# One store for each output row tile in place of two, and a later place for one pair's query sums, in an attention and FFN kernel

## The chip, the cores and the metric

One core of one Trainium2 chip. The metric is the device time of one execution in microseconds (us). A run that is over 1.5% above the fastest of its kernel is called slow and is left out of every ratio.

The span that a profile gives is some 1.8 us shorter than the time of the same run, because it goes from the first instruction to the last only. Differences of spans and differences of times can be put beside each other.

## The reference, cut to what matters

```python
# q, k, v: [8 batches, 8 heads, 1152, 64] f32
q_pool = q.reshape(B, H, S // 2, 2, D).mean(axis=3)           # 576 queries
attn   = softmax(q_pool @ k.T / 8)                            # 576 x 1152 for each head
x      = (attn @ v).transpose(0, 2, 1, 3).reshape(4608, 512)  # 8 x 576 tokens
out    = ((x @ w1) * (x @ w2)) @ w3 @ w_out                   # [4608, 512] f32
```

## The kernel before

The attention goes through the heads in 32 pairs, numbered from 0. For each pair TensorE forms the scores (`psc`, line 315), ScalarE the exponentials (`er`, line 325), and TensorE sums them with the values (`po`, line 340). VectorE divides (`xn`, line 357) and a DMA transposes the result into `xT` (lines 365 and 368). The keys and queries of pairs 8 to 31 come to TensorE by DMA transposes too: `kT<-kc` (line 145) and `qT<-qp` (line 148); those of pairs 0 to 7 are transposed by TensorE. All the DMA transposes are issued from SyncE, whose queue is called SP below. The loads of `q`, `k` and `v` are issued from GpSimd, but for the keys and queries of pair 0.

The second half of the reference runs in 9 units of 512 tokens. Seven of them are interleaved with the attention, so that TensorE has work while ScalarE is at the exponentials; two come at the end, with `tail` set. A unit forms two products (`pa`, `pb`, line 434), multiplies them (`gT`, line 446), and multiplies by `w3 @ w_out`, which is formed once (`T16`; `pp`, line 452). Then come four row tiles of 128 tokens: an eviction from the accumulator to `osb`, and a store.

The tokens of a batch are not in the order of the output's rows. Token `64*c + p` of a batch is output row `9*p + c`. So 64 neighbouring tokens go to rows that lie 9 apart, and a tile of 128 tokens is two such groups, `c` and `c + 1`. A tile that starts at token 512 of 576 reaches into the next batch.

```python
def rows(i, o, n):                      # columns o to o+n of row tile i of unit t
    def mm(p, ft):
        nc.tensor.matmul(p[:, 0:n], gT[:, ft, 128*i:128*i + 128], T16[:, ft, o:o + n],
                         start=(ft == 0), stop=(ft == NF - 1))
    def end(p):
        if o == 0:
            osbs[i] = ffp.tile([128, dm], FP32, tag="osb", bufs=6, name="osb")
        ...                             # evict p to osb, on ScalarE or VectorE
        if not final and o + n < dm:
            return
        cs = slice(o, o + n) if final else slice(0, dm)
        for z in range(2):
            b, f = divmod(t0 + 128*i + 64*z, SQ)
            dst = out[b*SQ:(b + 1)*SQ, :].rearrange("(p c) m -> c p m", c=NJ)
            eng = nc.scalar if final and z else nc.sync
            eng.dma_start(out=dst[f // 64][:, cs], in_=osbs[i][64*z:64*z + 64, cs])
    final = t == n_units - 1 and i == 3
    ...
for i in range(4):
    last = t == n_units - 1 and i == 3
    widths = (256, 128, 128) if last else (512,) if tail else (256, 256)
    ...

# in the loop over steps, where pairs 1 to 7 get their sums and copies on VectorE:
    if 5 <= staged < NPE and it >= first_it(staged) - 3:   # ahead of the step's matmul groups
        prep_stage(staged)                                 # qp = even + odd queries; kc = copy of keys
    ...                                                    # the groups of this step
    if staged < 5 and it >= first_it(staged) - 2:          # after them
        prep_stage(staged)
```

The softmax here doesn't subtract the row's maximum and nothing guards it: scores larger than these inputs give would overflow.

Of the kernel before, what the change touches and what calls it, by code (L numbers as in the profile page):

```python
# [14 lines left out]
SQ = 576  # L15
NJ = 9
# [7 lines left out]
def kernel(  # L24
# [11 lines left out]
    nc = tc.nc  # L36
    B, H, S, D = q.shape
    dm = H * D
# [6 lines left out]
    NPE = 8  # L45
# [13 lines left out]
    T16 = const.tile([128, NF, dm], FP16)  # L59
# [39 lines left out]
    def load(P):  # L99
        if P < NP:  # L100
            load_k(P)
            load_q(P)
            load_v(P)
# [32 lines left out]
    def prep_dma(P):  # L136

        pool_q(P, 2)
        for p in (P, P + 1):
            new_kq(p)  # L140
            nc.gpsimd.tensor_copy(  # L141
                out=new_kc(p).rearrange("p j u d -> p u j d").bitcast(mybir.dt.int32),
                in_=kst.pop(p).bitcast(mybir.dt.int32))
        for p in (P, P + 1):
            nc.sync.dma_start_transpose(
                out=kT[p], in_=kcs[p].rearrange("p j u d -> p (j u d)"))
            if p == P:
                nc.sync.dma_start_transpose(
                    out=qTs[P // 2], in_=qps[P // 2].rearrange("p c u d -> p (c u d)"))
# [12 lines left out]
    def prep_stage(P):  # L162

        pool_q(P)
        nc.vector.tensor_copy(out=new_kc(P).rearrange("p j u d -> p u j d"), in_=kst.pop(P))
# [135 lines left out]
    def scores(c):  # L301
        t = psum.tile([128, 2, CH], FP32, tag="psc", bufs=3, name="psc")
        psc[c] = t
        if 3 <= c < 10:
            nc.tensor.matmul(t[:, 0], ones[:, 0:128], ones, start=True, stop=True)
        g = c * CH
        while g < (c + 1) * CH:
            J = g // SQ
            P, j = divmod(J, NJ)
            f0 = g - J * SQ  # L310
            ln = min(SQ - f0, (c + 1) * CH - g)
            o = g - c * CH
            for u in range(2):
                s = slice(64 * u, 64 * u + 64)
                nc.tensor.matmul(t[:, u, o:o + ln].rearrange("p (c f) -> p c f", f=64), kT[P][s, j, :],  # L315
                                 qT[P][s, f0 // 64:(f0 + ln) // 64], start=True, stop=True)
            g += ln

    def expo(c):
        r = (c * CH) % RING  # L320
        g = (c - RING // CH + 1) * CH
        if g > 0:
            Pg, Jg = divmod((g - 1) // SQ, NJ)
            assert nb >= 90 * Pg + 45 + 5 * Jg + 5
        nc.scalar.activation(out=er[:, :, r:r + CH], in_=psc.pop(c), func=AF.Exp,  # L325
                             bias=0.0, scale=SCALE)
# [69 lines left out]
    tail = False  # L396
# [28 lines left out]
    def ffn_groups(t):  # L425
        t0 = 512 * t
        gT = ffp.tile([128, NF, 512], FP16, tag="g", name="gT")
        asb = {}

        def half(ft, name):  # L430
            w = w1sb if name == "pa" else w2sb

            def mm(p, mc):
                nc.tensor.matmul(p, w[:, mc, ft * 128:ft * 128 + 128],  # L434
                                 xT[:, mc, t0:t0 + 512],
                                 start=(mc == 0), stop=(mc == NC - 1))

            def end(p):
                if name == "pa":
                    asb[ft] = ffp.tile([128, 512], FP32, tag="asb", name="asb")  # L440
                    if tail:
                        nc.scalar.copy(out=asb[ft], in_=p)  # L442
                    else:
                        nc.vector.tensor_copy(out=asb[ft], in_=p)  # L444
                else:
                    nc.vector.tensor_mul(out=gT[:, ft, :], in0=p, in1=asb.pop(ft))  # L446
            return name, FP32, NC, mm, end

        def rows(i, o, n):

            def mm(p, ft):
                nc.tensor.matmul(p[:, 0:n], gT[:, ft, 128 * i:128 * i + 128],  # L452
                                 T16[:, ft, o:o + n],
                                 start=(ft == 0), stop=(ft == NF - 1))

            def end(p):
                if o == 0:
                    osbs[i] = ffp.tile([128, dm], FP32, tag="osb", bufs=6, name="osb")
                osb = osbs[i][:, o:o + n]
                if tail and not (final and o):  # L460
                    nc.scalar.activation(out=osb, in_=p[:, 0:n], func=AF.Copy, bias=0.0,  # L461
                                         scale=1.0 / (SCL * SCL))
                else:
                    nc.vector.tensor_scalar_mul(out=osb, in0=p[:, 0:n],  # L464
                                                scalar1=1.0 / (SCL * SCL))
                if not final and o + n < dm:
                    return
                cs = slice(o, o + n) if final else slice(0, dm)
                for z in range(2):
                    b, f = divmod(t0 + 128 * i + 64 * z, SQ)  # L470
                    dst = out[b * SQ:(b + 1) * SQ, :].rearrange("(p c) m -> c p m", c=NJ)
                    eng = nc.scalar if final and z else nc.sync
                    eng.dma_start(out=dst[f // 64][:, cs], in_=osbs[i][64 * z:64 * z + 64, cs])
            final = t == n_units - 1 and i == 3
            return "pp", FP32, NF, mm, end

        osbs = {}
        for ft in range(NF):
            yield half(ft, "pa")
            yield half(ft, "pb")  # L480
        for i in range(4):
            last = t == n_units - 1 and i == 3
            widths = (256, 128, 128) if last else (512,) if tail else (256, 256)
            for x, n in enumerate(widths):
                yield rows(i, sum(widths[0:x]), n)


    NCHUNK = NP * PAIR // CH
# [6 lines left out]
        out=ident, in_=ident, compare_op=ALU.not_equal, fill=1.0,  # L495
# [16 lines left out]
    loaded, staged, prepped, copied = 8, 1, 1, 1  # L512
# [24 lines left out]
    n_units = NT // 512  # L537
# [37 lines left out]
    def first_it(P):  # L575
        return P * PAIR // (CH * BURST)
# [21 lines left out]
    for it in range(NIT):  # L598
        at = it * BURST * CH / PAIR
        while early and it >= early[0][0]:  # L600
            queue.append(early.pop(0)[1])
        while next_unit < EARLY:
            last_b = (512 * (next_unit + 1) - 1) // SQ
            if it < 3 or reached[it - 2] < 360 * (last_b + 1):
                break
            gens.append(ffn_groups(next_unit))
            next_unit += 1
        for w in range(BURST):
            if it == 0 and w == 2:
                some()  # L610
            if it == 1 and w == 1:
                rest()
            scores(BURST * it + w)
            expo(BURST * it + w)
        if 5 <= staged < NPE and it >= first_it(staged) - 3:
            prep_stage(staged)
            staged += 1
        while 8 <= loaded < NPE + 2 and at >= loaded - 3.4:
            load(loaded)
            loaded += 1  # L620
        urgent = False
        if prepped < NPE:
            if it >= first_it(prepped) - (1 if prepped < 5 else 2):
                queue[0:0] = prep_groups(prepped)
                prepped += 1
                urgent = True
        elif prepped < NP and at >= prepped - 1.95:
            prep_dma(prepped)
            if loaded < NP:
                settled(prepped)  # L630
                load_two(loaded)
                loaded += 2
            prepped += 2
        if NPE <= copied < NP and at >= copied - 1.1:
            copy_v(copied)
            copied += 1
        n = PVS[it]
        left = 45 - nb % 45
        brief = bool(queue) and queue[0][2] == 1
        a = left if left < n else 8 if brief and it > 8 and 8 < n < 40 and 8 < left < 45 else 0  # L640
        assert nb + n <= NPV and ready(nb + n - 1, BURST * it)
        pv(a)
        if head():
            group("F")
        if head() and (n < 40 or urgent or it < 17):
            group("X")
        pv(n - a)
        if staged < 5 and it >= first_it(staged) - 2:
            prep_stage(staged)
            staged += 1  # L650
            more_loads(staged)
        if copied < NPE and at >= copied + (0.25 if copied < 5 else 0):
            copy_v(copied)
            copied += 1
        reached.append(nb)
# [6 lines left out]
    tail = True  # L662
# [36 lines left out]
```

## Time and profile before

| | before |
|---|---|
| time, median (lowest to highest) of the 3 runs there were at the prediction | 419.31 us (418.67 to 420.48) |
| span of the profiled run | 416.7 us |
| TensorE busy, from all of the span | 406.1 us, 97% |
| end of TensorE's last matmul | 411.28 us |
| stores of output, and their size | 73 from SP, 3 from ScalarE; 128 KB, fewer columns at the end |

TensorE bounds this kernel: it idles for 5.1 us in the first 110 us, in waits of at most 0.8 us each, for 0.02 us from there to 411.28, and then 5.4 us pass in which the last rows leave. The "DMA" row of the page gives the busy share of the 16 DMA engines in tenths.

### The profile page before, as it was taken

To read this page: it belongs to the slowest core of one execution; us is meant where nothing else is said; L and a number is where in the kernel's file an instruction comes from. 1 tells how busy PE (TensorE), PEld (TensorE's weight loads), DVE (VectorE), ACT (ScalarE), POOL (GpSimd) and SP (SyncE) were. 2 spreads that over 40 slices of the span, in tenths; PEclk is the share of its full clock that TensorE was granted. 3 is DMA by queue.
4 is the path that set the end of the run, shared out by engine and by line. 5 is a ranking of instruction groups with operands and counts; after the bars stand their busy time and mean duration, and the time that the engine had idled before them with its cause. 6 is when DMAs were issued, how large, how long until landed. Compare 5 with 4: busy or idle time off the path is not lost.

```text
span 416.7 us, 12724 instructions
## 1 busy us (share of the span) xinstructions
PE 406.1 (97%) x5497; PEld 270.6 (65%) x5497; DVE 197.1 (47%) x408; ACT 326.0 (78%) x356; POOL 120.9 (29%) x161
## 2 busy tenths in 40 slices
PE   8999999999999999999999999999999999999994
PEld 5677777766775577666856786668656866544442
DVE  3546666455445543544455644554555345613130
ACT  5999999889888899888888889898888998032331
POOL 6533431343535255243525205243430000000000
PEclk9999999999999999999999999999999999999999
DMA  8999999799999999999799949998993341050404
GB/s 199 202 203 192 188 205 195 113 158 154 155 189 205 178 172 180 185 149 182 147 216 143 167 92 197 137 161 146 192 183 62 56 78 31 2 116 2 101 2 102
DMA packets 96489, 59.76 MB, mean 143 GB/s; under 512 B 65584, under 2 KB 86704, under 8 KB 96432
## 3 DMA queue, kind: packets, MB, share of 16 engines
q0 software_dynamic: 26928, 32.97, 50.8%
q1 hardware_dynamic: 69264, 25.84, 36.5%
q8 instruction: 43, 0.70, 0.7%
q10 hardware_dynamic: 240, 0.13, 0.1%
q14 instruction: 14, 0.11, 0.1%
HBM read 67.11 MB, written 9.44 MB: 184 GB/s over the span
## 4 chain that ended last, share of the span: by engine, by line
PE 85%; DMA 10%; ACT 2%; POOL 1%; issue 1%; DVE 1%; ACTq 0%; POOLq 0%
PE po L340 19%; PE psc L315 17%; PE pa L434 16%; PE pp L452 16%; PE pb L434 15%; DMA qst<-in_q_dram 7%; DMA w3h<-in_moe_w_dram 2%; ACT er L325 2%; PE pT L418 2%; DMA er<-in_k_dram 1%; POOL kst L88 1%; PE t L169 0%; POOL vst L95 0%; DVE qp L121 0%; POOL qst L81 0%
## 5 line engine op out<-in xcount | busy, mean ns | idle before, releaser
L325 ACT ACTIVATE er<-psc 128x1024 f16<-128x1024 f32 x324 | 307.2, 1029 | 41.2 <-PE psc L315 41.1
L340 PEld LDWEIGHTS <-er 128*128 128x128 f16 x2880 | 103.3, 97 | 22.0 <-issue 5.9
L340 PE MATMUL po<-vt,er 128*128 128x65 f16 x2880 | 110.3, 193 | 0.0
L315 PE MATMUL psc<-qT,kT 64*128 64x512 f16 (+7 forms) x1152 | 95.0, 285 | 3.4 <-ACT er L325 2.0
L446 DVE TENSOR_TENSOR gT<-pb,asb 128x512 f16<-128x512 f32 x72 | 49.8, 691 | 56.0 <-PE pb L434 55.4
L434 PE MATMUL pa<-xT,w1sb 128*128 128x512 f16 x288 | 74.2, 380 | 0.0
L434 PE MATMUL pb<-xT,w2sb 128*128 128x512 f16 x288 | 74.1, 380 | 0.0
L452 PE MATMUL pp<-T,gT 128*128 128x256 f16 (+2 forms) x496 | 67.9, 290 | 0.0
L315 PEld LDWEIGHTS <-kT 64*128 64x128 f16 x1152 | 45.5, 94 | 28.2 <-issue 9.4
L452 PEld LDWEIGHTS <-gT 128*128 128x128 f16 x496 | 45.9, 98 | 18.4 <-issue 3.7
L444 DVE COPY asb<-pa 128x512 f32<-128x512 f32 x56 | 38.7, 691 | 39.7 <-PE pa L434 38.6
L434 PEld LDWEIGHTS <-w2sb 128*128 128x128 f16 x288 | 26.4, 98 | 32.7 <-issue 3.9
L434 PEld LDWEIGHTS <-w1sb 128*128 128x128 f16 x288 | 25.1, 98 | 30.1 <-issue 6.2
L121 POOL TENSOR_TENSOR qp<-qst 128x1152 f16<-128x1152 f16 x12 | 28.3, 2354 | 54.2 <-issue 28.2
L464 DVE TENSOR_SCALAR osb<-pp 128x256 f32<-128x256 f32 (+1 forms) x50 | 21.0, 419 | 39.0 <-PE pp L452 38.7
L353 DVE RECIPROCAL rz<-po 128x5 f32<-128x5 f32 x64 | 12.4, 194 | 48.0 <-PE po L340 47.6
L357 DVE TENSOR_TENSOR xn<-po,rz 128x320 f16<-128x320 f32 x64 | 31.5, 492 | 2.2
L141 POOL COPY kc<-kst 128x576 int32<-128x576 int32 x24 | 16.2, 677 | 54.4 <-issue 42.0
L95 POOL DMA_DIRECT2D vst<-in_v_dram x32 | 23.4, 742 | 13.7 <-DMA w3h<-in_moe_w_dram 4.3
L461 ACT ACTIVATE osb<-pp 128x512 f32<-128x512 f32 (+1 forms) x12 | 7.0, 579 | 24.0 <-PE pp L452 20.6
L88 POOL DMA_DIRECT2D kst<-in_k_dram x31 | 22.6, 745 | 8.2 <-DMA w1sb<-in_moe_w_dram 2.2
L442 ACT COPY asb<-pa 128x512 f32<-128x512 f32 x16 | 9.4, 585 | 16.5 <-PE pa L434 16.5
(49 smaller groups left out, 149.3 us busy)
## 6 DMA issues: line engine op xcount, KB each, us to landing
vst<-in_v_dram POOLq DMA_DIRECT2D x32, 288.0 KB, 10.4
out_dram<-osb SPq DMA_DIRECT2D x70, 128.0 KB, 2.5
qst<-in_q_dram POOLq DMA_DIRECT2D x31, 288.0 KB, 7.4
kst<-in_k_dram POOLq DMA_DIRECT2D x31, 288.0 KB, 12.5
w3h<-in_moe_w_dram POOLq DMA_DIRECT2D x3, 512.0 KB, 14.5
xT<-in_moe_w_out_dram POOLq DMA_DIRECT2D x4, 256.0 KB, 10.4
w1sb<-in_moe_w_dram POOLq DMA_DIRECT2D x2, 512.0 KB, 16.8
w2sb<-in_moe_w_dram POOLq DMA_DIRECT2D x2, 512.0 KB, 16.9
```

Of the source, the lines that this page charges most:

```text
L88: nc.gpsimd.dma_start(out=kst[P].rearrange("p u j d -> p u (j d)"), in_=k[b, h0:h0 + 2].rearrange("u (p j) d -> p u (j d)", j=NJ))
L95: nc.gpsimd.dma_start(out=vst[P].rearrange("p u j d -> p u (j d)"), in_=v[b, h0:h0 + 2].rearrange("u (p j) d -> p u (j d)", j=NJ))
L121: eng.tensor_tensor(out=qps[pp][r].rearrange("p c u d -> p u c d"), in0=src[:, :, :, 0, :], in1=src[:, :, :, 1, :], op=ALU.add)
L315: nc.tensor.matmul(t[:, u, o:o + ln].rearrange("p (c f) -> p c f", f=64), kT[P][s, j, :], qT[P][s, f0 // 64:(f0 + ln) // 64], start=True, ...
L325: nc.scalar.activation(out=er[:, :, r:r + CH], in_=psc.pop(c), func=AF.Exp, bias=0.0, scale=SCALE)
L340: nc.tensor.matmul(po[P, u][:, VW * x:VW * x + D + 1], er[:, u, r:r + 128], vts[P % 4][:, u, j, 0:D + 1], start=(m == 0), stop=(m == 44), ...
L357: nc.vector.tensor_tensor(out=xn[:, P % 2, :, u, :], in0=acc[:, :, 0:D], in1=rz.to_broadcast([128, 5, D]), op=ALU.mult)
L434: nc.tensor.matmul(p, w[:, mc, ft * 128:ft * 128 + 128], xT[:, mc, t0:t0 + 512], start=(mc == 0), stop=(mc == NC - 1))
L444: nc.vector.tensor_copy(out=asb[ft], in_=p)
L446: nc.vector.tensor_mul(out=gT[:, ft, :], in0=p, in1=asb.pop(ft))
L452: nc.tensor.matmul(p[:, 0:n], gT[:, ft, 128 * i:128 * i + 128], T16[:, ft, o:o + n], start=(ft == 0), stop=(ft == NF - 1))
L464: nc.vector.tensor_scalar_mul(out=osb, in0=p[:, 0:n], scalar1=1.0 / (SCL * SCL))
```

## The change

The intent is fewer DMA issues (41 stores in place of 76), a shorter end, and no wait in the step in which pair 5 is prepared. Its core, with the renaming of `rows(i, o, n)` to `rows(i, s, n)` (`o = n * s`) left out:

```diff
-                for z in range(2):
+                b, f = divmod(t0 + 128 * i, SQ)
+                if f + 128 <= SQ:
+                    dst = out[b * SQ:(b + 1) * SQ, :].rearrange("(p c) m -> c p m", c=NJ)
+                    nc.sync.dma_start(out=dst[f // 64:f // 64 + 2, :, cs], in_=osbs[i][:, cs])
+                    return
+                for z in range(2):              # a tile that reaches into the next batch
                     b, f = divmod(t0 + 128 * i + 64 * z, SQ)
                     dst = out[b * SQ:(b + 1) * SQ, :].rearrange("(p c) m -> c p m", c=NJ)
-                    eng = nc.scalar if final and z else nc.sync
-                    eng.dma_start(out=dst[f // 64][:, cs], in_=osbs[i][64 * z:64 * z + 64, cs])
+                    nc.sync.dma_start(out=dst[f // 64], in_=osbs[i][64 * z:64 * z + 64])
 ...
-            widths = (256, 128, 128) if last else (512,) if tail else (256, 256)
+            # the last tile: two halves of 256 columns; others of the tail 512; else 256 and 256
 ...
-        if 5 <= staged < NPE and it >= first_it(staged) - 3:
+        if 6 <= staged < NPE and it >= first_it(staged) - 3:
 ...
-        if staged < 5 and it >= first_it(staged) - 2:
+        if staged < 6 and it >= first_it(staged) - (2 if staged < 5 else 3):
```

Two lines with a `#` are this text's words for what the diff does there.

More of the change, by code (lines that the diff above doesn't have):

```diff
@@ L447, in half, with rows @@
             return name, FP32, NC, mm, end
-        def rows(i, o, n):
+        def rows(i, s, n):
             def mm(p, ft):
                 nc.tensor.matmul(p[:, 0:n], gT[:, ft, 128 * i:128 * i + 128],
-                                 T16[:, ft, o:o + n],
+                                 T16[:, ft, n * s:n * s + n],
                                  start=(ft == 0), stop=(ft == NF - 1))
             def end(p):
-                if o == 0:
+                if s == 0:
                     osbs[i] = ffp.tile([128, dm], FP32, tag="osb", bufs=6, name="osb")
-                osb = osbs[i][:, o:o + n]
-                if tail and not (final and o):
+                osb = osbs[i][:, n * s:n * s + n]
+                if tail and not (final and s):
                     nc.scalar.activation(out=osb, in_=p[:, 0:n], func=AF.Copy, bias=0.0,
@@ L465, in end @@
                                                 scalar1=1.0 / (SCL * SCL))
-                if not final and o + n < dm:
+                if not final and n * (s + 1) < dm:
                     return
-                cs = slice(o, o + n) if final else slice(0, dm)
+                cs = slice(n * s, n * s + n) if final else slice(0, dm)
+                b, f = divmod(t0 + 128 * i, SQ)
[3 more added lines that the diff above has]
+                    return
                 for z in range(2):
@@ L481, in ffn_groups @@
         for i in range(4):
-            last = t == n_units - 1 and i == 3
-            widths = (256, 128, 128) if last else (512,) if tail else (256, 256)
-            for x, n in enumerate(widths):
-                yield rows(i, sum(widths[0:x]), n)
+            if tail and not (t == n_units - 1 and i == 3):
+                yield rows(i, 0, 512)
+            else:
+                yield rows(i, 0, 256)
+                yield rows(i, 1, 256)
     NCHUNK = NP * PAIR // CH
```

## The prediction

> **What bounds the kernel now.** I read the page first (busy shares, the 40 slices, the chain that ended last), then the timeline of the last 12 us, then the DMA view of the same stretch and of 384 to 392 us, and last the timeline around 45 us, where pair 5 is prepared.
>
> ```profile
> span 416.7 us, 12724 instructions
> ...
> PE 406.1 (97%) x5497; PEld 270.6 (65%) x5497; DVE 197.1 (47%) x408; ACT 326.0 (78%) x356; POOL 120.9 (29%) x161
> ...
> PEclk9999999999999999999999999999999999999999
> DMA  8999999799999999999799949998993341050404
> ```
>
> TensorE is busy for 97% of the span at full clock, so 10.6 us of the span are open to any change that does not remove matmuls, and this one removes none of weight. The DMA row is the second thing to see: the 16 engines are at nine tenths until slice 30 or so (about 310 us). They are off the path, but they have little left.
>
> ```profile
> 403.96 7.15 PEld L452 LDWEIGHTS <-gT 128*128 128x128 f16 x48
> 404.17 7.11 PE L452 MATMUL pp<-T,gT 128*128 128x512 f16 x48
> ...
> 406.72 6.49 SPq L473 DMA_DIRECT2D out_dram<-osb  x9
> 407.82 0.60 ACT L461 ACTIVATE osb<-pp 128x512 f32<-128x512 f32 x1 [1.13 <-PE pp L452]
> ...
> 410.84 3.30 ACTq L473 DMA_DIRECT2D out_dram<-osb  x3
> 410.87 0.29 DVE L464 TENSOR_SCALAR osb<-pp 128x128 f32<-128x128 f32 x1 [5.74 <-PE pp L452]
> 411.32 0.29 DVE L464 TENSOR_SCALAR osb<-pp 128x128 f32<-128x128 f32 x1 [0.15 <-PE pp L452]
> ```
>
> The matmuls end at 411.28, the last eviction at 411.61, yet the span ends at 416.7: 5.1 us of store. ScalarE's queue issues three stores in a row until 414.14; by the stores' view its first issue alone took 1.73 us, and the third started at about 413.4. It landed 2.1 us after that start, at 415.5, and 1.2 us of closing follow.
>
> ```profile
> q1 hardware_dynamic: 720, 0.92, 33.3%
> q10 hardware_dynamic: 240, 0.13, 4.2%
> ...
> out_dram<-osb SPq DMA_DIRECT2D x6, 128.0 KB, 2.3
> out_dram<-osb ACTq DMA_DIRECT2D x1, 64.0 KB, 3.3
> out_dram<-osb SPq DMA_DIRECT2D x1, 64.0 KB, 2.0
> out_dram<-osb SPq DMA_DIRECT2D x2, 32.0 KB, 1.9
> out_dram<-osb ACTq DMA_DIRECT2D x2, 32.0 KB, 2.1
> ```
>
> This is the DMA view of 405 to 417. Count the packets: nine stores on the SP queue have 6x64 + 64 + 2x64 = 576 rows, and 720 - 576 = 144 = 9x16. So each store has 16 small packets beside its rows: one per DMA engine. Every store of now runs on all 16.
>
> ```profile
> q1 hardware_dynamic: 480, 0.79, 43.3%
> ```
>
> The same view of 384 to 392 us, six stores and nothing else: 43.3% of 16 x 8 us is 55.4 us, over 384 rows of 2 KB 144 ns each, with 16 engines writing together. The shortest 2 KB row among the trace's packet records is 81 ns, the shortest 1 KB row 44 ns.
>
> **What the Trainium skill says.** "DMA: Bandwidth & Descriptors", section "Why a DMA increments its semaphore by 16 and not by 1": a DMA is spread over k engines, where k is the largest number up to 16 that divides the size of the slowest dimension (other than 1) of both access patterns; the issuing queue uses the lowest-numbered k. The trace agrees for 64 rows on both sides (16 closing packets a store); no DMA of this kernel shows another k. The section "Queues, rings and completion order" of that page says that each engine consumes a queue's descriptors in ring order; no view here shows it directly. "Rules for kernel authors" of that page advises one 128-partition transfer in place of two on partition halves, which speaks for the change, and in another row warns that an outermost dimension under 16 confines the DMA to so many engines, which speaks against it.
>
> **The change part by part.**
>
> *The number of stores.* 36 row tiles; those that start at 512 of a 576-row batch (tiles 4, 13, 22, 31) keep two DMAs. 31 take one, the last two: 41 stores for 76. Some 35 issues at 0.47 to 0.6 us leave the SP queue, about 19 us, but TensorE waits for none of them (from 50 us on its waits are 0.9 us in all, on ScalarE). Worth: nothing.
>
> *The end, were stores as quick as now.* The 16 matmuls of 128 columns become 8 of 256. The two 128-wide evictions follow each other by 0.45 us, 55 ns a matmul, so the matmul time stays. The last eviction grows from 0.29 to 0.42 us (256 columns elsewhere take 425 ns) and ends at 411.74. The SP queue then has tile 34's store at 410.2, the first half at 410.85, the second at 411.78. It would land at 414.0 after 2.2 us, against 415.5, and the span would end at 415.2: 1.5 us saved, most of it the slow first issue on ScalarE's queue.
>
> *Pair 5's preparation.* In this step VectorE waits for pair 5's queries ahead of two evictions:
>
> ```profile
> 45.97 0.76 DVE L121 TENSOR_TENSOR qp<-qst 64x1152 f16<-64x1152 f16 x1 [1.44 <-DMA qst<-in_q_dram]
> ...
> 46.75 0.46 DVE L165 COPY kc<-kst 128x1152 f16<-128x1152 f16 x1
> ...
> 47.13 0.68 DVE L411 COPY w3T<-w3t 128x1024 f16<-128x1024 f16 x1
> ...
> 47.73 0.41 DVE L422 CAST T<-pT 128x256 f16<-128x256 f32 x1
> 48.20 0.39 PE L315 MATMUL psc<-qT,kT 64*128 64x512 f16 x2 [0.64 <-DVE T L422]
> ```
>
> TensorE loses 0.64 us to the buffer that the late eviction holds. Moved to the end, the sum runs at 46.8, its data being there since 45.94; the cast ends at 46.8 in place of 48.14 and the wait goes. ScalarE then takes up chunk 45 when chunk 44 is done, at 50.29 in place of 50.79. I count 0.5 us, which lasts because the steps up to 76 us hand over between TensorE and ScalarE. Its data for the next step is ready at 47.9, before the transposes want it at 48.3.
>
> *How the one DMA is spread.* The new destination is a pattern of 2 x 64 x 512: two groups of rows 512 elements apart, 64 rows in each 9x512 apart. No two of these dimensions merge. The source has 128 partitions. The largest number that divides 2 and 128 is 2. If the rule holds, each new store runs on two engines, always the same two, 64 rows on each instead of 4. One tile then takes 64 x 81 to 144 ns = 5.2 to 9.2 us, a half tile 64 x 44 ns = 2.8 us or more.
>
> At the end: tile 32's rows start some 1.2 us after their issue, at 407.9, and then come in one line tiles 32, 33, 34 (15.6 us) and the two halves (5.6): 429.1, and with 0.4 for the last notice and 1.2 of closing 430.7. That is 14 us over now; with the longer rows (3 x 9.2 and 2 x 4.6) 31 us.
>
> In the middle: from 110 to 310 us, by the packet records, an engine has 96 us of load packets (10230 x 106 ns and 2386 x 192 ns, over 16), 48 us of transposes (42419 x 18 ns) and 15 us of stores (2560 x 96 ns), taken at their medians: 159 of 200 us. 20 tiles fall in it, 18 of them single: on the two engines the stores become 18 x 64 x 82 to 96 ns = 94 to 111 us, the total 240 to 256 us. The two engines are short by 40 to 56 us, and each load and transpose has a share on them. Key transposes stand in the same ring behind the stores, and the loads wait for them. Some is absorbed: pairs are loaded about two ahead (20 us), and after 310 us the engines are half idle. I count 30 us, from 0 to 90.
>
> Sum in this case: 419.3 + 14 to 20 + 30 = about 465, from 432 to 540.
>
> **The rivals.** (a) *Two engines*, as just told. For it: the rule's wording, the dimension of 2, the engines that are full until 310. Against it: no DMA of now has a leading dimension under 16, and a tuned kernel would hardly be given such a store. (b) *Sixteen engines*: the split goes by rows after all. Then 1.5 + 0.5 us are saved: 417.3. For it: the advice for one 128-partition transfer, and the 5.1 us tail that it shortens. (c) *Two engines, but only the end suffers*: the rings drain between units (43 us apart, 4 x 5.2 = 21 us of stores in each), TensorE never waits, and it ends at about 433. (d) *A slower row*: two engines write 2 KB rows at 144 ns or more, the middle is short by 100 us, and output buffers (six) hold up the evictions: over 520.
>
> **Range and chances.** I give (b) a quarter, (a) with (c) and (d) nearly three quarters. The middle of that mixture lies near 455; the range has to reach from just under (b) to most of (a): 416 to 520. Faster by over 2% would need 8.4 us, and all the idle time of TensorE is 10.6: 0.03. Within 2%: 0.25. Slower: 0.72.
>
> **What would show it.** Packets: with two engines, a store of 128 rows has 2 closing packets and not 16, and lands 6 us or more after its issue instead of 2.3; with sixteen it lands in about 2.5. The end: from the last matmul to the end 3.9 us (b) or about 19 (a). The middle: waits of TensorE on transposes or on VectorE's output evictions, of GpSimd on key transposes, and a later end of the loads than 310. Around 48 us: no wait of the scores on the cast. I am wrong if the store lands within 3 us, and wrong in size if TensorE stays at full load between 110 and 350 us.

## The result, and the profile after

| | before | after |
|---|---|---|
| time, median (lowest to highest) of 4 runs | 418.99 us (418.07 to 420.48) | 480.54 us (477.82 to 496.53) |
| span of the profiled run | 416.7 us | 476.0 us |
| TensorE busy | 406.1 us | 416.9 us |
| end of the last matmul | 411.28 us | 455.16 us |
| from there to the end of the span | 5.4 us | 20.9 us |

The kernel became slower: ratio 1.144 (95% interval 1.135 to 1.153). This ratio, and each one below, is the mean time of one kernel's fast runs over that of the other's in the same rounds, so it is not quite the ratio of the medians. The run of 496.53 us was slow and is not in it.

The page of the kernel after: busy time by engine, the rows of 40 slices (11.9 us each), and the stores.

```profile
span 476.0 us, 12658 instructions
...
PE 416.9 (88%) x5489; PEld 275.6 (58%) x5489; DVE 197.8 (42%) x407; ACT 325.9 (68%) x356; POOL 120.9 (25%) x161
...
PE   8999999999995899689995999379995999999920
...
PEclk9999999999999799979999899879999999999975
DMA  8999997999979999999949999399999571111211
...
out_dram<-osb SPq DMA_DIRECT2D x31, 256.0 KB
...
out_dram<-osb SPq DMA_DIRECT2D x10, 128.0 KB
```

The first twelve slices of the PE row are as they were. The first store is issued at 111 us, in the tenth slice, and from the thirteenth on the row has holes, with lower digits of the granted clock beside them. In the kernel before they were solid nines:

```profile
PE   8999999999999999999999999999999999999994
```

The DMA row stays near nine until some 370 us (310 before), and ends in a row of ones.

The same is seen by stage. These are busy times by engine in stretches of the kernel before (columns: length, then PE, PEld, DVE, ACT, POOL with the instructions in brackets, granted clock, DMA share, GB/s):

```profile
0.00:110.00 110.00, 104.86 (x1641) 75.80 (x1642) 59.01 (x134) 97.37 (x105) 45.07 (x68) 1.00 1.10 179
110.00:310.00 200.00, 199.98 (x2872) 136.58 (x2870) 98.12 (x200) 173.08 (x183) 75.17 (x92) 1.00 1.08 169
310.00:350.00 40.00, 40.00 (x592) 27.84 (x591) 19.55 (x41) 35.52 (x39) 0.67 (x1) 1.00 0.39 67
```

and of the kernel after:

```profile
0.00:110.00 110.00, 104.79 (x1642) 75.63 (x1643) 59.27 (x134) 97.35 (x106) 45.27 (x68) 1.00 1.10 181
110.00:310.00 200.00, 175.47 (x2420) 118.25 (x2419) 84.29 (x170) 146.49 (x154) 58.32 (x71) 0.95 1.09 132
310.00:350.00 40.00, 36.96 (x476) 24.52 (x476) 16.84 (x35) 29.27 (x31) 13.63 (x19) 0.93 1.04 135
350.00:411.00 61.00, 55.56 (x743) 36.63 (x742) 25.92 (x52) 37.71 (x41) 3.69 (x3) 0.97 0.69 80
```

Until 110 us the two kernels are alike. From 110 to 310 us TensorE is busy for 24.5 us less and does 452 matmuls fewer. A trap lies in the last two columns: the DMA share is the same in both, 1.08 and 1.09, while the bytes moved fall from 169 to 132 GB/s. A packet's time seems to count its waiting too: the longest packet of 256 bytes took 14.5 us here and 2.0 us before, with the same median of 18 ns. So read the share together with the GB/s. The work of the loads then goes on past 310 us, at 135 GB/s where the kernel before had 67.

What ended the waits is the next view. Of the kernel after (total us, times, longest):

```profile
ACT er L325 <- PE psc L315: 84.9, 94, 10.4
...
POOL seen L152 <- DMA kT<-kc: 58.5, 11, 10.6
...
PE po L340 <- issue: 20.6, 3, 9.6
...
DVE xn L357 <- DMA xT<-xn: 14.3, 3, 7.0
...
PE po L340 <- DVE xn L357: 10.9, 2, 6.1
```

In the kernel before the first two were 41.1 and 39.4 us, and the other three are not among its waits. GpSimd issues the loads, and it waits for the key transposes before it issues more (the little copy `seen`); so late transposes mean late loads. One wait reads like this in the timeline of the kernel after (start, duration, engine, line, operation, count, idle before it and what ended that):

```profile
136.80 13.85 SPq L365 DMA_TRANSPOSE xT<-xn  x2
...
146.65 1.53 PE L340 MATMUL po<-vt,er 128*128 128x65 f16 x45
...
148.87 1.04 PE L434 MATMUL pb<-xT,w2sb 128*128 128x512 f16 x4
150.70 1.23 SPq L368 DMA_TRANSPOSE xT<-xn  x1
...
155.43 0.49 DVE L357 TENSOR_TENSOR xn<-po,rz 128x320 f16<-128x320 f32 x1 [7.01 <-DMA xT<-xn]
...
155.97 2.65 PE L340 MATMUL po<-vt,er 128*128 128x65 f16 x45 [6.07 <-DVE xn L357]
```

VectorE wants to write `xn`, but the transposes that read its older contents are still in the SP queue: their two issues took 13.85 us together, where one such issue takes 1.3 us in the median and at most 2.3 us in the kernel before. The accumulator `po` has one buffer, so TensorE waits 6.07 us for VectorE. Then the same group of 45 matmuls takes 2.65 us in place of 1.53. The Trainium skill, "TensorE: Matmul & The Clock Gate", section "Part 1: The HAM clock gate (the "warmup" mystery)", says that the clock falls to half after one or more windows of about 3.4 us without work and comes back after one or more such windows at work. The trace agrees: 1.73 times the duration after a gap of 6.07 us; its clock records have half the clock from 155.1 to 161.9 us, so 5.2 us after the work stopped and until 6.0 us after it went on. Over the span the mean granted clock is 0.950, against 0.998.

In the later part the chain that ended last runs through the loads of keys. Part of it, in the kernel after (start, duration, what):

```profile
255.54 5.66 DMA kT<-kc
...
276.77 6.75 DMA kT<-kc
...
287.46 25.12 DMA kst<-in_k_dram
312.59 3.92 DMA kT<-kc
...
320.46 11.99 DMA kst<-in_k_dram
...
333.18 6.20 SPq L145
...
339.43 6.62 DMA qT<-qp
```

A key load took 25 us, the transposes 4 to 7 us, and an issue of a transpose was held for 6.2 us. What that long load ran into is seen in the DMA view of 286 to 309 us (40 slices of 0.575 us):

```profile
DMA  0999899999999911111111111111111111118999
GB/s 10 254 218 214 152 153 164 203 177 173 200 177 101 38 33 35 37 33 41 33 34 37 33 41 33 37 35 35 35 37 35 37 33 45 48 46 131 179 179 180
```

For 12.7 us, from 294.0 to 306.7, the share is between one and two tenths: the work of some two engines of 16, while loads and transposes are pending. And last the end, in the timeline of the kernel after:

```profile
450.62 15.41 SPq L472 DMA_DIRECT2D out_dram<-osb  x5
...
454.32 0.38 ACT L461 ACTIVATE osb<-pp 128x256 f32<-128x256 f32 x1 [0.28 <-PE pp L452]
455.19 0.42 DVE L464 TENSOR_SCALAR osb<-pp 128x256 f32<-128x256 f32 x1 [6.16 <-PE pp L452]
```

and in its DMA view of 456 to 476 us:

```profile
DMA  1111111111111111111111111111111111110000
...
q1 hardware_dynamic: 577, 0.90, 11.9%
```

11.9% of 16 engines is 1.9 engines: two engines' worth of writing until 474 us, at about 50 GB/s, and fourteen stand still. The packet records agree. After 450 us there are five stores, with 640 row packets and 10 small closing ones, so two for each store where a store of the kernel before had 16. A row of 2 KB took 84 ns in the median and one of 1 KB 46 ns.

Taken together, the span grew by 59.3 us. The last matmul ends 43.9 us later; 33.1 of that is idle time of TensorE (455.16 - 416.9 against 411.28 - 406.1) and 10.8 is longer busy time. The clock records account for the latter: TensorE works for 22.3 us at half clock (none in the kernel before), which would make 11.2 us. The end after the last matmul grew by 15.4 us.

### The profile page after: what moved, and what is told of

It is laid out like the page before. It is cut to its first block, busy times and chain, and to the rows that moved or that the text cites. A ratio compares the mean times of both kernels' runs of the same rounds, so it can differ in the third digit from the quotient of the medians.

```text
span 476.0 us, 12658 instructions
## 1 busy us (share of the span) xinstructions
PE 416.9 (88%) x5489; PEld 275.6 (58%) x5489; DVE 197.8 (42%) x407; ACT 325.9 (68%) x356; POOL 120.9 (25%) x161
## 4 chain that ended last, share of the span: by engine, by line
PE 65%; DMA 17%; ACT 5%; issue 4%; SPq 2%; POOL 2%; DVE 1%; ACTq 0%; POOLq 0%; DVEq 0%
PE po L340 14%; PE psc L315 13%; PE pa L434 11%; PE pb L434 11%; PE pp L452 11%; DMA kst<-in_k_dram 9%; ACT er L325 5%; DMA kT<-kc 3%; PE pT L418 2%; DMA qT<-qp 1%; SPq L145 1%; DMA er<-in_k_dram 1%; DMA xT<-xn 1%; DMA qst<-in_q_dram 1%; POOL vst L95 1%
## 5 line engine op out<-in xcount | busy, mean ns | idle before, releaser
L340 PE MATMUL po<-vt,er 128*128 128x65 f16 x2880 | 114.6, 196 | 31.6 <-issue 20.6
L340 PEld LDWEIGHTS <-er 128*128 128x128 f16 x2880 | 106.9, 99 | 55.1 <-issue 27.5
L315 PE MATMUL psc<-qT,kT 64*128 64x512 f16 (+7 forms) x1152 | 97.7, 291 | 4.5 <-ACT er L325 2.7
L434 PE MATMUL pa<-xT,w1sb 128*128 128x512 f16 x288 | 75.9, 387 | 0.0
L452 PE MATMUL pp<-T,gT 128*128 128x256 f16 (+1 forms) x488 | 68.9, 295 | 0.0
L464 DVE TENSOR_SCALAR osb<-pp 128x256 f32<-128x256 f32 x49 | 20.8, 425 | 40.0 <-PE pp L452 40.0
L81 POOL DMA_DIRECT2D qst<-in_q_dram x31 | 19.2, 621 | 9.7 <-DMA vst<-in_v_dram 2.8
## 6 DMA issues: line engine op xcount, KB each, us to landing
vst<-in_v_dram POOLq DMA_DIRECT2D x32, 288.0 KB, 11.2
```

The source lines that it names most:

```text
L315: nc.tensor.matmul(t[:, u, o:o + ln].rearrange("p (c f) -> p c f", f=64), kT[P][s, j, :], qT[P][s, f0 // 64:(f0 + ln) // 64], start=True, ...
L340: nc.tensor.matmul(po[P, u][:, VW * x:VW * x + D + 1], er[:, u, r:r + 128], vts[P % 4][:, u, j, 0:D + 1], start=(m == 0), stop=(m == 44), ...
L434: nc.tensor.matmul(p, w[:, mc, ft * 128:ft * 128 + 128], xT[:, mc, t0:t0 + 512], start=(mc == 0), stop=(mc == NC - 1))
L452: nc.tensor.matmul(p[:, 0:n], gT[:, ft, 128 * i:128 * i + 128], T16[:, ft, n * s:n * s + n], start=(ft == 0), stop=(ft == NF - 1))
L464: nc.vector.tensor_scalar_mul(out=osb, in0=p[:, 0:n], scalar1=1.0 / (SCL * SCL))
```

## The experiments

Two theories stood against each other at first. *Two engines*: the destination pattern of the merged store, 2 x 64 x 512, leads with a 2, so that two DMA engines do all of it, and everything that shares these two falls behind. *Large stores*: one DMA of 128 rows scattered over the output is itself what hurts, or the pair 5 part. Later a question within the first theory came up: are the transposes late because they stand behind the stores in the SP queue, or because the two engines are full, whichever queue asks?

### Same size, another leading dimension: 128 neighbouring rows

```diff
-  dst = out[b * SQ:(b + 1) * SQ, :].rearrange("(p c) m -> c p m", c=NJ)
-  nc.sync.dma_start(out=dst[f // 64:f // 64 + 2, :, cs], in_=osbs[i][:, cs])
+  r0 = t0 + 128 * i
+  nc.sync.dma_start(out=out[r0:r0 + 128, cs], in_=osbs[i][:, cs])
```

The kernel after, with rows put in the wrong places; some rows of the output stay unwritten.

> The changed kernel with one edit: a merged store writes 128 neighbouring output rows (a wrong row order, on purpose), so that its destination leads with a dimension of 128 and not of 2. Still 41 stores, the same bytes, the same end, pair 5 moved. Theory 'two engines' (the leading 2 confines a store to two DMA engines): the whole loss goes, about 417.3 us (416.5 to 418.5), 16 closing packets a store, landing in about 2.5 us. Rival 'merging' (one store of 256 KB in place of two, or the simpler end, costs the time): it stays at 470 to 485.

Measured: 416.40 us, ratio 0.993 (0.990 to 0.995). The DMA view of the last stretch, 404 to 420 us:

```profile
q1 hardware_dynamic: 720, 1.05, 18.0%
...
out_dram<-osb SPq DMA_DIRECT2D x3, 256.0 KB, 2.0
out_dram<-osb SPq DMA_DIRECT2D x2, 128.0 KB, 1.7
```

720 packets are 5 x 128 rows and 5 x 16 closing ones: sixteen engines. A store of 256 KB lands in 2.0 us. Size and number of the stores are as in the kernel after, and the loss is gone. But the rows are also contiguous now, so this alone does not tell the leading dimension from the scatter; the next two do.

### The same two groups of rows, with 64 as the leading dimension

The order of the tokens within a tile can be chosen when `gT` is written, because each of its columns becomes an output row. Written so that tokens `p` of both groups lie side by side, one store can lead with `p`:

```diff
-  nc.vector.tensor_mul(out=gT[:, ft, :], in0=p, in1=asb.pop(ft))
+  nc.vector.tensor_mul(
+      out=gT[:, ft, :].rearrange("k (i p c) -> k i c p", i=4, c=2),
+      in0=p.rearrange("k (i c p) -> k i c p", i=4, c=2),
+      in1=asb.pop(ft).rearrange("k (i c p) -> k i c p", i=4, c=2))
...
-  dst = out[b * SQ:(b + 1) * SQ, :].rearrange("(p c) m -> c p m", c=NJ)
-  nc.sync.dma_start(out=dst[f // 64:f // 64 + 2, :, cs], in_=osbs[i][:, cs])
+  dst = out[b * SQ:(b + 1) * SQ, :].rearrange("(p c) m -> p c m", c=NJ)
+  nc.sync.dma_start(out=dst[:, f // 64:f // 64 + 2, cs], in_=osbs[i][:, cs])
...
-  nc.sync.dma_start(out=dst[f // 64], in_=osbs[i][64 * z:64 * z + 64])
+  nc.sync.dma_start(out=dst[f // 64], in_=osbs[i].rearrange("(p c) m -> c p m", c=2)[z])
```

The result is right.

> The changed kernel, right result, with the row order inside a tile turned round when the products are written (row p of both groups next to each other), so that one store of 128 rows has a destination that leads with 64. Theory 'two engines': 16 engines a store, about 417.3 us, a ratio of 0.995 to before, if VectorE's strided write costs nothing on the path. Rival 'merging': 470 to 485. If the strided write is slow on VectorE (half idle), up to 1 us more.

Measured: 417.36 us, ratio 0.994 (0.992 to 0.997), with the same bytes to the same rows by the same 41 stores as the kernel after. This version is the quickest right one. Its five last stores have 720 packets again (view of 404 to 420 us), so 16 closing ones each, and in its stretch from 110 to 310 us TensorE has no holes:

```profile
q1 hardware_dynamic: 720, 1.05, 17.8%
```

```profile
110.00:310.00 200.00, 199.75 (x2862) 136.42 (x2859) 99.35 (x200) 172.53 (x183) 74.94 (x92) 1.00 1.11 170
```

From the last matmul to the end 3.91 us pass, as expected. The strided write of `gT` takes 736 ns in place of 691, which adds no wait.

### The old stores, led by 2

The reverse: the kernel before, with its 76 stores of 64 rows, each split into a leading dimension of `a = 2`.

```diff
-  eng.dma_start(out=dst[f // 64][:, cs], in_=osbs[i][64 * z:64 * z + 64, cs])
+  eng.dma_start(out=dst[f // 64].rearrange("(p a) m -> a p m", a=2)[:, :, cs],
+                in_=osbs[i][64 * z:64 * z + 64, cs])
```

The rows of a group come out in another order. The comparison with the reference passed nevertheless: within a batch the output's rows differ by 8.8e-8 (standard deviation), beside 8.9e-6 over the whole output, so it does not see such an order. (For the version with 64 leading, the order was therefore checked apart, by simulating both kernels with `q` and `k` 15 times as large, so that rows differ: relative error 0.0011, against 1.38 for this one.)

> The kernel before with one edit: each of the two 64-row stores of a tile writes its rows as 2 groups of 32 (a wrong row order, on purpose), so that the destination leads with 2; still 76 stores, nothing merged, nothing else moved. Theory 'two engines': as slow as the changed kernel, 470 to 495 us, with 2 closing packets a store. Rival 'merging': as before, 419.

Measured: 501.01 us, ratio 1.194 (1.190 to 1.198), a little over the upper end. Nothing is merged in it, so neither the number of the stores nor their size makes the loss. It is larger than in the kernel after by 20.5 us, which fits with the four tiles that reach into the next batch: they also run on two engines here, 4 x 64 rows x 84 ns = 21.5 us of work on each of the two. TensorE's waits in this kernel are mostly those on VectorE's `xn` (41.6 us, five of them) and on `qT` transposes (5.3 us).

### The dose: 4 and 8

The same edit with `a = 4` and `a = 8`.

> As the two-store run with groups of 32 rows, but 4 groups of 16 (a wrong row order): 4 engines a store if the rule holds, two stores a tile, so 32 rows of 84 ns = 2.7 us of an engine per tile. Theory 'two engines are full': from 110 to 310 us an engine had 144 us of loads and transposes; with 20 x 2.7 = 54 us of stores 198 of 200, just full, so a small loss in the middle (0 to 15 us) and some 5 us at the end: 422 to 440. 4 closing packets a store. Rival (any store on few engines blocks the queue alike): near 480.

> The same with 8 groups of 8 rows (a wrong row order): 8 engines a store, 16 rows or 1.35 us of an engine per tile, 144 + 27 = 171 of 200 us. Theory: 419 to 424, with 2 us at the end at most. 8 closing packets a store.

Three of the stores are alone on ScalarE's queue in these kernels, with 64 rows each, so that queue's packet count gives the number of engines. With a = 2, 4 and 8, in this order:

```profile
q10 hardware_dynamic: 198, 0.13, 0.1%
```

```profile
q10 hardware_dynamic: 204, 0.13, 0.1%
```

```profile
q10 hardware_dynamic: 216, 0.13, 0.1%
```

192 rows and 3 x 2, 3 x 4, 3 x 8 closing packets; 240 were 3 x 16 in the kernel before. Up to 16, the leading dimension is the number of engines. The times:

| engines per store | median time, us | ratio to before | from the last matmul to the end, us | busy time of one of the shared engines, 110 to 310 us, estimated |
|---|---|---|---|---|
| 16 (before) | 419 | 1 | 5.4 | 159 |
| 8 | 421.32 | 1.006 | 7.1 | 171 |
| 4 | 444.00 | 1.062 | 12.1 | 198 |
| 2 | 501.01 | 1.194 | 22.3 | 252 |

The last column is the prediction's estimate: 144 us of loads and transposes on each engine, and for the stores of 20 tiles 1280, 640 or 320 rows of 84 ns, with 15 us at 16 engines. With 8 engines the sum still fits into 200 us, and the loss is little more than the longer end. With 4 it is just full, TensorE's busy time in that stretch falls to 189.87 us, and the time came out 4 us above what was expected. With 2 it can't fit. By this estimate the loss starts where the fullest engine runs out of time.

### Half the bytes

Is it time on the engine, or something fixed in a DMA on two engines? The merged stores of the kernel after, each of half its columns (a wrong result):

```diff
+                    cs = slice(cs.start, (cs.start + cs.stop) // 2)
                     nc.sync.dma_start(out=dst[f // 64:f // 64 + 2, :, cs], in_=osbs[i][:, cs])
```

> The changed kernel, but a merged store writes only half of its columns (a wrong result, the rest stays unwritten): still two engines, still 64 rows on each, at 46 ns in place of 84: 2.9 us per tile, the same engine time as the run with 4 groups. Theory 'time on the engine counts': 425 to 445, near the run with 4 groups. Rival (the number of engines or of rows counts): above 460.

Measured: 435.69 us, ratio 1.042 (1.036 to 1.048). Rows of 1 KB take 46 ns, so 18 tiles make 18 x 64 x 46 ns = 53 us for each of the two engines, the same sum as with four engines above (54), and the loss of 4.2% lies near that one's 6.2% and far from the 14.4% of the kernel after, with as many rows on as few engines. So the time that the rows take on the two engines counts, and not their number or a fixed cost of such a DMA.

### The end alone, and the middle alone

```diff
-                if f + 128 <= SQ:
+                if f + 128 <= SQ and t >= EARLY:      # the end alone
```

> The changed kernel with the single store only in the two units of the tail (row tiles 28 to 35); the first seven units store each tile by two 64-row DMAs on 16 engines. Theory: only the end suffers; TensorE ends as in the changed kernel without its middle (411), then five stores stand in line on two engines, 3 x 5.4 + 2 x 2.9 us, from about 408 on: end at 431, time 433 to 435. Rival (the loss is in the middle alone): 418 to 420.

Measured: 433.85 us, ratio 1.035 (1.032 to 1.038). The last matmul ends at 410.87 us, and 21.0 us pass after it.

```diff
-                if f + 128 <= SQ:
+                if f + 128 <= SQ and t < EARLY:       # the middle alone
```

(and the split stores write the columns `cs` alone, so that the last tile's halves come out right)

> The changed kernel with the single store only in the first seven units; the tail's two units store by two 64-row DMAs on 16 engines. Theory: the changed kernel's 480.5 less the 15 us of its end: 463 to 467, with the waits of TensorE between 148 and 368 us as in the changed kernel. Rival (middle and end are one backlog, so that neither part alone costs its share): below 450.

Measured: ratio 1.116 (1.109 to 1.124) from its two fast runs, 466.40 and 470.36 us; two others were slow, the profiled one among them. That reaches above what was expected. The two parts together make 1.035 + 1.116 - 1 = 1.151, inside the interval of the whole: the end and the middle are separate losses.

### Pair 5 alone

```diff
-        if 5 <= staged < NPE and it >= first_it(staged) - 3:
+        if 6 <= staged < NPE and it >= first_it(staged) - 3:
...
-        if staged < 5 and it >= first_it(staged) - 2:
+        if staged < 6 and it >= first_it(staged) - (2 if staged < 5 else 3):
```

> The kernel before with pair 5's query sums and key copies at the step's end, and nothing else. My working: 0.5 us saved, ratio 0.9988, the 0.64 us wait of the scores on the cast at 48 us gone. Rival: later waits eat it, ratio 1.000; or it is slower, which would be a part of the loss.

Measured: 418.42 us, ratio 0.997 (0.995 to 1.000). The wait of the scores for the cast is gone from the trace (0.64 us before, none in this run's list of waits), and the gain is between nothing and half a per cent; runs of this kind can't tell 0.5 us from 1.

### Queue order or full engines: the stores on ScalarE's queue

The prediction had the transposes stand "in the same ring behind the stores". If that is what hurts, stores issued from another engine should help. A control does the same to the version with 64 leading.

```diff
-                    nc.sync.dma_start(out=dst[f // 64:f // 64 + 2, :, cs], in_=osbs[i][:, cs])
+                    nc.scalar.dma_start(out=dst[f // 64:f // 64 + 2, :, cs], in_=osbs[i][:, cs])
```

(and the stores of the tiles that reach into the next batch likewise)

> The changed kernel with its output stores issued on ScalarE's queue in place of the SP queue: still two engines a store, but the transposes no longer stand behind them in one ring. Theory 'ring' (the middle is lost because transposes wait in line behind the stores): most of the 44 us of the middle goes, 435 to 445 plus what the control shows ScalarE's issues to cost. Theory 'two engines are full' (loads and transposes have a share on them, whatever the ring): it stays within 10 us of 480.

> Control for the run before: the sixteen-engine kernel (one store a tile, destination leading with 64) with its stores on ScalarE's queue. ScalarE waits in order for VectorE's evictions before each issue, 41 issues of 0.6 to 0.7 us: 417.4 and up to 12 us more where exponentials come later; ScalarE is idle 13% of the middle, so I expect 419 to 424. The difference of the run before from this one is what two engines cost without the shared ring.

Measured: 528.64 us with two engines as the median of four runs, two of them slow (fast runs 521.15 and 527.15; ratio 1.249, 1.240 to 1.259), and 424.14 us for the control (1.013, 1.008 to 1.018). Both theories' numbers missed: it became slower still. The SP queue of the two-engine kernel, which held no store at all now (timeline; the profiled run was slow, but the fast ones are far above the control too):

```profile
241.76 7.36 SPq L148 DMA_TRANSPOSE qT<-qp  x1
...
243.65 5.53 ACTq L472 DMA_DIRECT2D out_dram<-osb  x1
244.32 1.93 ACT L325 ACTIVATE er<-psc 128x1024 f16<-128x1024 f32 x2
...
249.62 8.64 SPq L145 DMA_TRANSPOSE kT<-kc  x1
```

The transposes' issues are still held for 7 to 9 us, with no store ahead of them in their queue. So standing behind stores in the SP queue is not needed for the loss. It fits with two engines that are full for both queues, but no view here names the engine of a packet. The Trainium skill, "DMA: Bandwidth & Descriptors", section "Issuing engines are not separate DMA queues", says that DMAs from any issuing engine run on the same 16, which agrees with the held issues here. The additional loss fits with ScalarE's own issues, which were held too (5.53 us in the line shown; ten of them for 2.6 us or more), and ScalarE has the exponentials to do. How much of the additional 45 us (means of the fast runs, against the kernel after) that makes was not measured apart.

### What stays open

Of TensorE's idle time in the kernel after, 20.6 us are three stalls on "issue", for which the trace shows no semaphore:

```profile
203.55 0.93 PE L340 MATMUL po<-vt,er 128*128 128x65 f16 x14 [5.55 <-issue]
...
311.62 0.32 PE L340 MATMUL po<-vt,er 128*128 128x65 f16 x3 [9.64 <-issue]
...
367.16 1.59 PE L340 MATMUL po<-vt,er 128*128 128x65 f16 x26 [5.44 <-issue]
```

They lie a multiple of 256 instructions of TensorE apart (2560 and 1280), and its program comes by DMA in pieces of that size: queue q8 of the trace has 43 packets of 16 KB, and 43 x 256 = 11008 is about the number of TensorE's instructions (10,991 in the trace). For the longest stall the packets show the delay. In the kernel before, the k-th piece starts when TensorE has done between k - 0.35 and k + 0.27 times 256 instructions; in the kernel after, the 31st starts only at 31.75 times 256, where TensorE stands. It lands at 310.25 us, after a stretch in which no such packet was moved (285.8 to 309.2) for 12.7 us of which only some two engines worked, and TensorE goes on 1.4 us later. In the run with 4 engines two stalls of 3.4 and 3.5 us lie at such places too and end 1.5 us after such a packet. By this order in time the program itself was late, for 9.6 of the 20.6 us. For the other two stalls no piece arrives just before they end; they end 0.5 us after the last row of a backlog of stores. What held them stays open, and no run here takes any of the three away.

That loads, transposes and program share the stores' two engines is inferred, from the closing packets, the dose series and the stretches in which the work of two engines is left.

## Why the prediction was right

*The spread over two engines* held to the letter: two closing packets for a merged store, and in the dose series 2, 4, 8 and 16 engines for a leading dimension of 2, 4, 8 and 64. The rival "sixteen engines" was a fair picture of what the store would do with another leading dimension: it said 417.3 us, and the version that leads with 64 took 417.36.

*The end* was said to grow by 14 us, at 81 ns a row of 2 KB; it grew by 15.4, and by 14.7 us of time where the end alone was changed. The 19 us from the last matmul on were 20.9. The version with longer rows (31 us; its own terms sum to 29.6) fell: two engines writing alone took 84 ns, and the 144 ns of the kernel before belong to 16 engines writing together.

*The middle* was said to cost 30 us, and the last matmul came 43.9 us later. The 30 us were thought of as waiting, and the idle time of TensorE grew by 33.1; the term that was left out is the slower clock after each wait. Groups of the same matmuls have longer means by 1 to 2% in the page (the `po` ones 196 ns against 193, the scores 291 against 285), and the busy time grew by 10.8 us. So the term was mis-sized by a third of its true size, most of it the clock. That the waiting alone came so near is partly luck: only 12 us of it are waits of TensorE on VectorE's `xn` and on a `qT` transpose, the kind of wait that was forecast, and 20.6 us are the stalls on "issue", of which the prediction has nothing.

*The way of the wait* was half right. The transposes and, through them, the loads were late, as told (GpSimd's waits on key transposes grew from 39.4 to 58.5 us). But it does not take a place behind the stores in one ring: with the stores in another queue the issues were held as well, for 7 to 9 us.

*Pair 5* was said to save 0.5 us: its sum and cast moved as told, and alone it measured 0 to 0.5%, which agrees and proves little. *The end with quick stores*, 1.5 us saved: 5.44 to 3.91 us in the version that leads with 64.

*The number itself*, 455, was not any case's. Two engines alone made 465, and the sum with the measured terms is 419.3 + 15.4 + 43.9 = 478.6. A quarter of chance for sixteen engines pulled the stated time down by another ten; the range up to 520 covered what came.

## What to carry to other kernels

When several DMAs are merged into one, look at the leading dimension of both patterns, and count the closing packets of one store in the trace: here a leading dimension of 2, 4 or 8 put the whole transfer on so many engines. What that costs hung here on how full those engines were already: 8 of 16 engines cost 0.6%, 4 cost 6%, and 2 cost 14 to 19%, with no change in bytes. The cure was to change the order in which an earlier instruction writes (45 ns each, hidden), so that the large dimension could lead.

## What the Trainium skill lacked or had wrong

- "DMA: Bandwidth & Descriptors", "Rules for kernel authors": the row that advises one 128-partition transfer in place of two partition halves stands without a condition; the one on the leading dimension is in another row of the table. Followed with a pattern that leads with 2 it cost 61 us of 419; with one that leads with 64 it gained 2.
- The same page doesn't say that a full engine holds the issuing engine itself. In the kernel after, issues of `xT` transposes on SP took up to 15.5 us (2.3 at most before), of stores up to 9.7 us (2.0 before), and with the stores on ScalarE's queue up to 5.5 us there. That the full engine is what holds them is inferred.
- The same page, section "Issuing engines are not separate DMA queues", calls the issue time usually small relative to the DMA. That holds for the kernel before (0.6 us in the median for a store that lands after 2.5 us) and not for the kernel after, where issues of transposes took up to 15.5 us.
- No page has the time of a store's rows by the number of engines writing: 84 ns for 2 KB and 46 ns for 1 KB with two engines, and 144 ns for 2 KB with 16 together.
- "Runtime: NRT & Kernel Launch" treats the DMA of an engine's own program, but has no figure for what it costs when that DMA falls behind on busy engines: one late piece of TensorE's program went with a stall of 9.6 us here. Two more such stalls, 11.0 us together, stay unexplained.
